# Inputs in 4 KB pieces and transposes of 32-bit token pairs in a recurrent gate kernel

## The chip, the cores and the metric

The kernel runs on one core of one Trainium2 chip. The metric is device time in microseconds, as the median of the executions of one kernel. Each execution carries a state: in these single-core runs, "slow" marks one that is more than 1.5% above the fastest of the same kernel. Ratios below are the mean time of one kernel's fast runs over that of the other kernel's fast runs of the same rounds, on the same chip; so they are not quite the ratio of the medians that stand beside them.

## The reference

Four sequences of 6336 tokens, 256 channels, all in float32. Cut to what matters:

```
a    = exp(8 * sigmoid(r_gate) * log(sigmoid(a_param)))     # decay
norm = sqrt(max(1 - a*a, 1e-6))
xg   = norm * sigmoid(i_gate) * x
h_t  = a_t * h_(t-1) + xg_t                                 # scan over tokens
gate = sigmoid(causal 5-tap convolution of h)
out  = (gate * (h @ w_val)) @ w_out
```

## The kernel before

Tokens come in chunks of 1024 (two tiles of 512). Loads lay tokens on the partitions; the scan needs channels there. So ACT takes tanh of the two gates; DVE or POOL (GpSimd) forms u = (1 + tanh i) * x, called u2 in the text; PE transposes the r half; ACT takes exp of it to give `a`; POOL squares `a` ("e"); ACT takes the root ("sq", several chunks at once); PE transposes the norm back to tokens (nT); DVE multiplies it with u (xg); PE transposes that (xT); and DVE scans it. Loads and stores go on SyncE's queue (called the load queue here), the small weights on GpSimd's software queue.

```
U2 = "PDPDDDDDDPDPDPDPDDPDPPPPPPPPPPPPPPPDPPPPPPPDPPPPPPP"   # who makes u2 of each tile: POOL or DVE
...
def load(c):       # r in pieces of 4 KB (j tokens side by side), i in pieces of 1 KB; x like i
    nc.sync.dma_start(ri[:, 0, 0:nw, 0:nj, :], rf[...].rearrange("(w p j) d -> p w j d", w=nw, j=nj))
    nc.sync.dma_start(ri[:, 1, ...], if_[...].rearrange("(k p) d -> p k d", p=P))
...
nc.vector.tensor_scalar(out=wo[:], in0=wo[:], scalar1=0.5, ...)          # setup, DVE's last instruction there
...
def op_u2(g, eng):
    xt, ti = live["xt", c][:, w * nj:(w + 1) * nj, :], tring[:, NTR + g % NTI, 0:nj, :]
    u = uring[:, g % NU, 0:nj, :]
    if eng == "DVE":
        nc.vector.scalar_tensor_tensor(out=u, in0=ti, scalar=1.0, in1=xt, op0=ALU.add, op1=ALU.mult)
        return
    nc.gpsimd.tensor_scalar(out=t1, in0=ti, ...)                         # t1 = 1 + tanh, f32
    nc.gpsimd.tensor_tensor(out=u, in0=t1, in1=xt, op=ALU.mult)
...
def op_nT(g, eng):                                                       # 8 bf16 transposes a tile
    for h in range(H):
        for j in range(nt // P):
            nc.tensor.transpose(out=nT[:, j, h*P:(h+1)*P], in_=nring[:, h, n0+j*P:n0+(j+1)*P], identity=ident_b[:])
```

The order of the instructions on each engine isn't written down: a small planner in the kernel simulates the engines with a table of costs (`COST`, us per operation) and emits the operations in order of their planned start.

## Time and profile before

| | before |
|---|---|
| median of the 3 runs | 319.87 us (317.4 to 322.94) |
| profiled span, granted clock | 317.1 us, 0.973 |
| ACT busy / idle | 290.1 / 27.0 us |
| POOL busy; in the 120 us from 120 to 240 us | 224.6 us; 114.3 us, 95% |
| share of the load queue (all 16 engines' span) | 91.8% |

The busy table, the stretches, the groups and the windows of the DMA are shown in the prediction. The view of the tile ring that holds u (duration in ns: least/median/most; then first and last start in us):

```profile
L404 DVE TENSOR_TENSOR uring<-bank,uring x51: 398/684/695, 14.6 to 306.2; 128x1024 bf16<-128x1024 bf16 x48, 128x512 bf16<-128x512 bf16 x3
L364 POOL TENSOR_TENSOR uring<-t,xt x36: 1264/2366/3320, 11.3 to 290.2; 128x1024 bf16<-128x1024 f32 x33, 128x512 bf16<-128x512 f32 x3
L360 DVE SCALAR_TENSOR_TENSOR uring<-tring,xt x15: 1198/1381/2480, 24.3 to 265.8; 128x1024 bf16<-128x1024 bf16 x15
```

The first xg starts at 14.6 us: until then DVE has nothing of the main loop to do: it waits for PE's first transposes of the norm, not for `wo`. Then two rows of the waits (engine, line, what it waited for; us in total, times, longest):

```profile
DVE uring L404 <- PE bank L397: 11.6, 15, 4.1
...
DVE wo L313 <- DMA wo<-in_moe_w_out_dram: 7.1, 1, 7.1
```

The second is the setup's scaling of the output weights `wo`. DVE works in order, so everything behind it waits as well.

### The profile page before, as it was taken

The page shows a single profiled execution, that of the slowest core. Times are in us where ns is not written, and L with a number is a line of the kernel's source. Part 1 is how long each engine was busy: PE and PEld are TensorE (multiplying, and loading weights), DVE is VectorE, ACT ScalarE, POOL GpSimd, SP SyncE. Part 2 cuts the span into 40 slices and gives each one's busy share as a digit, 9 for nine tenths or more (in the row PEclk, how much of TensorE's full clock was granted, in tenths as well). Part 3 has the DMA queues.
Part 4 walks back from the last instruction along what each step waited for, and adds up shares of the span by engine and source line. Part 5 has one row for each costly group of instructions (what it writes and reads, how often), then busy time and mean ns, then how long its engine had stood idle before and what let it go on. Part 6 is the DMA issues. An engine that isn't in the chain of part 4 may idle for free.

```text
span 317.1 us, 7227 instructions
## 1 busy us (share of the span) xinstructions
PE 246.2 (78%) x2987; PEld 163.6 (52%) x2987; DVE 270.4 (85%) x269; ACT 290.1 (91%) x231; POOL 224.6 (71%) x140
## 2 busy tenths in 40 slices
PE   1262877687679768897989798959977997999994
PEld 1141745453546446564655375627644665655662
DVE  3125799999597998999999999997998999999892
ACT  6789999899969999999998999899989999998963
POOL 6329551869469536999989999999997289868000
PEclk9999999999759999999999999997999999999997
DMA  8999999999999999999999999996999994853334
GB/s 208 340 365 380 367 368 382 386 345 352 394 322 349 389 356 375 350 391 385 357 382 382 393 369 383 393 389 191 395 385 383 385 379 164 262 189 133 135 154 179
DMA packets 67327, 104.55 MB, mean 330 GB/s; under 512 B 3287, under 2 KB 54238, under 8 KB 67294
## 3 DMA queue, kind: packets, MB, share of 16 engines
q1 hardware_dynamic: 65904, 103.82, 91.8%
q0 software_dynamic: 1376, 0.26, 1.0%
q8 instruction: 23, 0.38, 0.5%
q14 instruction: 10, 0.08, 0.1%
q10 hardware_dynamic: 14, 0.01, 0.0%
HBM read 78.39 MB, written 25.95 MB: 329 GB/s over the span
## 4 chain that ended last, share of the span: by engine, by line
ACT 25%; DMA 23%; DVE 21%; PE 13%; issue 10%; POOL 4%; SPq 1%; DVEq 0%; ACTq 0%; POOLq 0%
DMA ri<-in_i_gate_dram 15%; DVE yring L425 9%; ACT tring L351 8%; DMA xt<-in_x_dram 6%; DVE gv L477 5%; ACT ering L388 5%; PE bank L489 4%; ACT tg L459 4%; ACT aring L376 4%; PE gp L451 3%; DVE osb L500 3%; PE bank L397 3%; POOL uring L364 2%; DMA ri<-in_r_gate_dram 2%; DVE uring L404 2%
## 5 line engine op out<-in xcount | busy, mean ns | idle before, releaser
L384 POOL TENSOR_TENSOR ering<-aring 128x1024 f32<-128x1024 f32 (+2 forms) x56 | 97.1, 1753 | 55.0 <-ACT aring L376 52.8
L425 DVE TENSOR_TENSOR_SCAN yring<-aring,yring,bank 128x1024 bf16<-128x1024 f32 (+5 forms) x54 | 110.1, 2052 | 0.7 <-PE bank L332 0.5
L351 ACT ACTIVATE tring<-ri 128x2048 bf16<-128x2048 f32 (+1 forms) x51 | 93.9, 1868 | 7.8 <-DMA ri<-in_i_gate_dram 7.7
L364 POOL TENSOR_TENSOR uring<-t,xt 128x1024 bf16<-128x1024 f32 (+1 forms) x36 | 83.6, 2323 | 9.9 <-DMA xt<-in_x_dram 7.3
L451 PE MATMUL gp<-yring,diag 64*64 64x512 bf16 (+14 forms) x1196 | 67.9, 350 | 6.7 <-ACT tg L459 4.6
L489 PE MATMUL bank<-wo,gv 128*128 128x256 bf16 x396 | 57.3, 279 | 18.5 <-DVE gv L477 8.2
L477 DVE SCALAR_TENSOR_TENSOR gv<-tg,val 128x1024 bf16<-128x1024 bf16 (+1 forms) x54 | 60.3, 1120 | 6.7 <-ACT tg L459 4.5
L376 ACT ACTIVATE aring<-bank,khf 128x1024 f32<-128x1024 bf16 (+2 forms) x56 | 59.6, 1111 | 3.3 <-PE bank L332 2.5
L459 ACT ACTIVATE tg<-gp 128x1024 bf16<-128x1024 f32 (+1 forms) x51 | 51.1, 1003 | 7.1 <-PE gp L451 6.8
L489 PEld LDWEIGHTS <-gv 128*128 128x128 bf16 x396 | 36.0, 99 | 37.9 <-issue 16.4
L467 PE MATMUL val<-yring,wv 128*128 128x512 bf16 (+1 forms) x204 | 51.5, 376 | 0.8 <-DVE gv L477 0.8
L500 DVE COPY osb<-bank 128x512 f32<-128x512 f32 x69 | 45.6, 679 | 3.8 <-PE bank L489 3.3
L451 PEld LDWEIGHTS <-diag 64*64 64x64 bf16 x1196 | 30.9, 108 | 33.0 <-issue 16.5
L388 ACT ACTIVATE ering<-ering,b 128x2048 bf16<-128x2048 f32 (+4 forms) x15 | 46.7, 3112 | 0.3
L332 PE MATMUL bank<-ident_b,tring 128*128 128x128 bf16 x396 | 31.3, 231 | 18.5 <-ACT tring L351 13.0
L397 PE MATMUL bank<-ident_b,ering 128*128 128x128 bf16 x396 | 32.9, 240 | 15.8 <-ACT ering L388 12.5
L404 DVE TENSOR_TENSOR uring<-bank,uring 128x1024 bf16<-128x1024 bf16 (+1 forms) x51 | 33.4, 669 | 11.8 <-PE bank L397 11.6
L363 POOL TENSOR_SCALAR t<-tring 128x1024 f32<-128x1024 bf16 (+1 forms) x36 | 40.1, 1115 | 2.6 <-ACT tring L351 1.2
L397 PEld LDWEIGHTS <-ering 128*128 128x128 bf16 x396 | 28.1, 108 | 23.3 <-ACT ering L388 15.5
L332 PEld LDWEIGHTS <-tring 128*128 128x128 bf16 x396 | 25.7, 103 | 27.7 <-ACT tring L351 15.1
L332 PE MATMUL bank<-ident_b,uring 128*128 128x128 bf16 x396 | 30.4, 226 | 3.3 <-DVE yring L425 1.8
L360 DVE SCALAR_TENSOR_TENSOR uring<-tring,xt 128x1024 bf16<-128x1024 bf16 x15 | 24.4, 1624 | 8.2 <-DMA xt<-in_x_dram 8.2
(32 smaller groups left out, 112.6 us busy)
## 6 DMA issues: line engine op xcount, KB each, us to landing
out_dram<-osb SPq DMA_DIRECT2D x48, 512.0 KB, 7.1
ri<-in_r_gate_dram SPq DMA_DIRECT2D x23, 1024.0 KB, 8.1
ri<-in_i_gate_dram SPq DMA_DIRECT2D x23, 1024.0 KB, 11.8
xt<-in_x_dram SPq DMA_DIRECT2D x23, 1024.0 KB, 10.7
ri<-in_r_gate_dram SPq DMA_DIRECT2D x2, 512.0 KB, 5.9
ri<-in_i_gate_dram SPq DMA_DIRECT2D x2, 512.0 KB, 8.1
xt<-in_x_dram SPq DMA_DIRECT2D x2, 512.0 KB, 8.1
ri<-in_r_gate_dram SPq DMA_DIRECT2D x3, 256.0 KB, 2.9
```

Source lines behind the costliest of these rows:

```text
L332: nc.tensor.transpose(out=dst[:, col:col + P], in_=src[:, j, h * P:(h + 1) * P], identity=ident_b[:])
L351: nc.scalar.activation(out=tring[:, r:i + 1:i - r, 0:nj, :], in_=ri[:, :, w, 0:nj, :], func=ACT.Tanh, scale=0.5)
L364: nc.gpsimd.tensor_tensor(out=u, in0=t1, in1=xt, op=ALU.mult)
L376: nc.scalar.activation(out=aring[:, h, a0:a0 + nt].rearrange("c (w p j) -> c w p j", p=P, j=nj), in_=live.pop(("srT", k))[:, 0:nt].rearran ...
L384: nc.gpsimd.tensor_tensor(out=ering[:, h, e0:e0 + nt], in0=a, in1=a, op=ALU.mult)
L388: nc.scalar.activation(out=nring[:, :, 2 * e0:2 * e0 + m], in_=ering[:, :, e0:e0 + m], func=ACT.Sqrt, scale=-0.25, bias=b025[:, 0:1])
L397: nc.tensor.transpose(out=nT[:, j, h * P:(h + 1) * P], in_=nring[:, h, n0 + j * P:n0 + (j + 1) * P], identity=ident_b[:])
L425: nc.vector.tensor_tensor_scan(out=yring[:, h, y0 + c0:y0 + c1], data0=aring[:, h, a0 + c0:a0 + c1], data1=xT[:, c0:c1], initial=0.0 if fr ...
L451: nc.tensor.matmul(out=gp[64 * h:64 * h + 64, m, c0:c1], lhsT=diag[rows, h, kk, rows], rhs=yring[rows, h, src:src + c1 - c0], start=(sh == 0),
L459: nc.scalar.activation(out=tg[:, :, 0:nt], in_=live.pop(("gp", g))[:, :, 0:nt], func=ACT.Tanh, scale=0.5)
L477: nc.vector.scalar_tensor_tensor(out=gv[:, 0:nj, hs, :].rearrange("c j h p -> c j (h p)"), in0=tg[:, hs, 0:nt].rearrange("c h (p j) -> c j ...
L489: nc.tensor.matmul(out=ops[:, e * D:(e + 1) * D], lhsT=gv[:, 2 * i + e, hk, :], rhs=wo[:, hk, :], start=(hk == 0), stop=(hk == H - 1))
```

## The change

The intent: i_gate and x, too, come in pieces of 4 KB. Then one partition holds four neighbouring tokens, and a pair of neighbouring bf16 tokens can be taken as one 32-bit word: half as many transposes, in f32, and no copying. For this u must hold the two tokens of a pair side by side, while tanh and x lie token by token. The change lets u2 do the interleaving: it reads both its inputs with hops (512 or 1024 bytes at every element) and writes in a row. The core of the diff:

```diff
-COST = dict(load=(0.05, 2.8), loadx=(0.02, 1.5), ..., u2P=(0.25, 3.15), u2D=(0.2, 1.55), ..., store=(0.05, 1.3))
+COST = dict(load=(0.05, 2.72), loadx=(0.02, 1.37), ..., u2P=(0.25, 3.4), u2D=(0.3, 1.75), ..., store=(0.05, 1.33))
...
-        nc.sync.dma_start(xt[:, 0:nt // P, :], xf[...].rearrange("(k p) d -> p k d", p=P))
+        nc.sync.dma_start(xt[:, 0:nw, 0:nj, :], by_token(xf, c))      # "(w p j) d -> p w j d"; i_gate likewise
...
+            xt = live["xt", c][:, w, 0:nj, :].rearrange("p (w e) d -> p w d e", e=2)
+            u = uring[:, g % NU, 0:nj * D].rearrange("p (w d e) -> p w d e", d=D, e=2)
             if eng == "DVE":
-                nc.vector.scalar_tensor_tensor(out=u, in0=ti, scalar=1.0, in1=xt, ...)
+                tk = ti.rearrange("p (w e) d -> p w d e", e=2)
+                for k in range(nj // 2):
+                    nc.vector.scalar_tensor_tensor(out=u[:, k], in0=tk[:, k], scalar=1.0, in1=xt[:, k], ...)
...
-            nc.gpsimd.tensor_tensor(out=u, in0=t1, in1=xt, op=ALU.mult)
+            nc.gpsimd.tensor_tensor(out=u, in0=t1.rearrange("p (w e) d -> p w d e", e=2), in1=xt, op=ALU.mult)
...
-                for j in range(nt // P):
-                    nc.tensor.transpose(out=nT[:, j, h*P:(h+1)*P], in_=nring[:, h, ...], identity=ident_b[:])
+                for w in range(nw):
+                    nc.tensor.transpose(out=nT[:, w*D + h*P:...], in_=ering[:, h, n0 + w:n0 + nw*P:nw], identity=ident_f[:])
```

The transposes of xg (xT) change in the same way. The table of costs is edited along with it.

More of the change, by code (lines that the diff above doesn't have):

```diff
@@ L36 @@
 U2 = "PDPDDDDDDPDPDPDPDDPDPPPPPPPPPPPPPPPDPPPPPPPDPPPPPPP"
-COST = dict(load=(0.05, 2.8), loadx=(0.02, 1.5), tanh=(0.2, 1.7), u2P=(0.25, 3.15), u2D=(0.2, 1.55), srT=(0.05, 0.45), exp=(0.35, 0.86), e=(0.1, 1.8),
+COST = dict(load=(0.05, 2.72), loadx=(0.02, 1.37), tanh=(0.2, 1.7), u2P=(0.25, 3.4), u2D=(0.3, 1.75), srT=(0.05, 0.45), exp=(0.35, 0.86), e=(0.1, 1.8),
             sq=(0.3, 1.71), nT=(0.05, 0.47), xg=(0.1, 0.58), xT=(0.05, 0.45), scan=(0.21, 2.14), conv=(0.2, 1.1), tg=(0.19, 0.83),
             val=(0.02, 0.93), gv=(0.15, 1.07), out=(0.02, 0.47), osbD=(0.68, 0), osbA=(0.59, 0),
-            store=(0.05, 1.3))
+            store=(0.05, 1.33))
 PRIO = dict(load=5.92, loadx=5.97, store=2.53, tanh=6, exp=2.8, sq=0.42, tg=-0.32, srT=-1.6, nT=0.31, xT=3.79,
@@ L242, with by_token @@
     live = {}
+    def by_token(src, c):
+        t0, nt, g0, g1 = chunks[c]
+        return src[t0:t0 + nt, :].rearrange("(w p j) d -> p w j d", w=g1 - g0, p=P)
     def load(c):
@@ L247, in load @@
         ri = inp.tile([P, 2, 2, SUB, D], FP32, name="ri", tag="ri", bufs=NIN)
-        nc.sync.dma_start(ri[:, 0, 0:nw, 0:nj, :], rf[t0:t0 + nt, :].rearrange("(w p j) d -> p w j d", w=nw, j=nj))
-        nc.sync.dma_start(ri[:, 1, 0:nw, 0:nj, :].rearrange("p w j d -> p (w j) d"),
-                          if_[t0:t0 + nt, :].rearrange("(k p) d -> p k d", p=P))
+        nc.sync.dma_start(ri[:, 0:nw, 0, 0:nj, :], by_token(rf, c))
+        nc.sync.dma_start(ri[:, 0:nw, 1, 0:nj, :], by_token(if_, c))
         live["ri", c] = ri
@@ L255, in loadx @@
         t0, nt, g0, g1 = chunks[c]
-        xt = inp.tile([P, 2 * SUB, D], FP32, name="xt", tag="xt", bufs=NX)
-        nc.sync.dma_start(xt[:, 0:nt // P, :], xf[t0:t0 + nt, :].rearrange("(k p) d -> p k d", p=P))
+        nw, nj = g1 - g0, nt // (g1 - g0) // P
+        xt = inp.tile([P, 2, SUB, D], FP32, name="xt", tag="xt", bufs=NX)
+        nc.sync.dma_start(xt[:, 0:nw, 0:nj, :], by_token(xf, c))
         live["xt", c] = xt
@@ L317, with bank @@
         psum = ctx.enter_context(tc.tile_pool(name="psum", bufs=1, space=bass.MemoryType.PSUM))
-        def bank(b, dtype):
+        def bank(b, dtype=FP32):
             return psum.tile([P, WIN * 4 // mybir.dt.size(dtype)], dtype, name=f"bank{b}", tag=f"bank{b}", bufs=1)
@@ L324 @@
         tring = rings.tile([P, NTR + NTI, SUB, D], BF16, name="tring")
-        uring = rings.tile([P, NU, SUB, D], BF16, name="uring")
+        uring = rings.tile([P, NU, SUB * D], BF16, name="uring")
+        uring_w = uring[:].bitcast(FP32)
         yring = rings.tile([P, H, NY * WIN], BF16, name="yring")
-        def transposes(dst, srcs, h):
-            col = 0
-            for src, nj in srcs:
-                for j in range(nj):
-                    nc.tensor.transpose(out=dst[:, col:col + P], in_=src[:, j, h * P:(h + 1) * P],
-                                        identity=ident_b[:])
-                    col += P
         def op_load(g, eng):
@@ L350, in op_tanh @@
             r, i = g % NTR, NTR + g % NTI
-            nc.scalar.activation(out=tring[:, r:i + 1:i - r, 0:nj, :], in_=ri[:, :, w, 0:nj, :], func=ACT.Tanh, scale=0.5)
+            nc.scalar.activation(out=tring[:, r:i + 1:i - r, 0:nj, :], in_=ri[:, w, :, 0:nj, :], func=ACT.Tanh, scale=0.5)
         def op_u2(g, eng):
@@ L356, in op_u2 @@
             w = g - chunks[c][2]
-            xt, ti = live["xt", c][:, w * nj:(w + 1) * nj, :], tring[:, NTR + g % NTI, 0:nj, :]
-            u = uring[:, g % NU, 0:nj, :]
+            xt = live["xt", c][:, w, 0:nj, :].rearrange("p (w e) d -> p w d e", e=2)
+            ti = tring[:, NTR + g % NTI, 0:nj, :]
+            u = uring[:, g % NU, 0:nj * D].rearrange("p (w d e) -> p w d e", d=D, e=2)
             if eng == "DVE":
-                nc.vector.scalar_tensor_tensor(out=u, in0=ti, scalar=1.0, in1=xt, op0=ALU.add, op1=ALU.mult)
+                tk = ti.rearrange("p (w e) d -> p w d e", e=2)
+                for k in range(nj // 2):
+                    nc.vector.scalar_tensor_tensor(out=u[:, k], in0=tk[:, k], scalar=1.0, in1=xt[:, k], op0=ALU.add,
+                                                   op1=ALU.mult)
                 return
@@ L368, in op_srT @@
             srT = bank(banks["srT", k], BF16)
-            transposes(srT, [(tring[:, g % NTR], tiles[g][1] // P) for g in range(*chunks[c][2:])], h)
+            col = 0
+            for g in range(*chunks[c][2:]):
+                for j in range(tiles[g][1] // P):
+                    nc.tensor.transpose(out=srT[:, col:col + P], in_=tring[:, g % NTR, j, h * P:(h + 1) * P],
+                                        identity=ident_b[:])
+                    col += P
             live["srT", k] = srT
@@ L392, in op_nT @@
             c = chunk_of[g]
-            n0, nt = shape.npos[c] + tiles[g][0] - chunks[c][0], tiles[g][1]
-            nT = bank(banks["nT", g], BF16)[:].rearrange("p (j d) -> p j d", d=D)
+            n0, nw = (shape.npos[c] + tiles[g][0] - chunks[c][0]) // 2, tiles[g][1] // P // 2
+            nT = bank(banks["nT", g])
             for h in range(H):
-                for j in range(nt // P):
-                    nc.tensor.transpose(out=nT[:, j, h * P:(h + 1) * P],
-                                        in_=nring[:, h, n0 + j * P:n0 + (j + 1) * P], identity=ident_b[:])
+                for w in range(nw):
+                    nc.tensor.transpose(out=nT[:, w * D + h * P:w * D + (h + 1) * P],
+                                        in_=ering[:, h, n0 + w:n0 + nw * P:nw], identity=ident_f[:])
             live["nT", g] = nT
         def op_xg(g, eng):
-            nj = tiles[g][1] // P
-            u = uring[:, g % NU, 0:nj, :]
-            nc.vector.tensor_tensor(out=u, in0=live.pop(("nT", g))[:, 0:nj, :], in1=u, op=ALU.mult)
+            n = tiles[g][1] // P * D
+            u = uring[:, g % NU, 0:n]
+            nc.vector.tensor_tensor(out=u, in0=live.pop(("nT", g))[:].bitcast(BF16)[:, 0:n], in1=u, op=ALU.mult)
         def op_xT(k, eng):
             c, h = k // 2, k % 2
-            xT = bank(banks["xT", k], BF16)
-            transposes(xT, [(uring[:, g % NU], tiles[g][1] // P) for g in range(*chunks[c][2:])], h)
+            xT = bank(banks["xT", k])
+            at = 0
+            for g in range(*chunks[c][2:]):
+                nw = tiles[g][1] // P // 2
+                for w in range(nw):
+                    nc.tensor.transpose(out=xT[:, at + w:at + nw * P:nw],
+                                        in_=uring_w[:, g % NU, w * D + h * P:w * D + (h + 1) * P], identity=ident_f[:])
+                at += nw * P
             live["xT", k] = xT
@@ L422, in op_scan @@
             yp = yend(c) - 1
-            xT = live.pop(("xT", k))
+            xT = live.pop(("xT", k))[:].bitcast(BF16)
             for (c0, c1, fresh) in shape.segments(t0, nt):
@@ L485, in op_out @@
             gv = live["gv", g]
-            ops = bank(banks["out", q], FP32)
+            ops = bank(banks["out", q])
             for e in range(2):
```

## The prediction

> **What bounds the kernel now.** I read the page's busy table first, then the busy time of each engine in stretches of 20 us, then the DMA view of two short windows, then the groups, and the chain of waits last.
>
> ```profile
> span 317.1 us, 7227 instructions
> ...
> PE 246.2 (78%) x2987; PEld 163.6 (52%) x2987; DVE 270.4 (85%) x269; ACT 290.1 (91%) x231; POOL 224.6 (71%) x140
> ```
>
> Four engines are near full on average. Only ACT is so full that its own work nearly is the time: 317.1 - 290.1 = 27.0 us idle. The stretches say when (columns: busy us of PE, weight loads, DVE, ACT, POOL; then granted clock, DMA share, GB/s).
>
> ```profile
> core 0: us, PE busy (x) PEld busy (x) DVE busy (x) ACT busy (x) POOL busy (x), PEclk, DMA share, GB/s
> 0.00:20.00 20.00, 6.07 (x47) 3.77 (x47) 5.45 (x23) 14.44 (x16) 10.02 (x18) 1.00 1.02 296
> ...
> 60.00:80.00 20.00, 14.94 (x180) 8.76 (x180) 18.16 (x15) 18.11 (x13) 15.63 (x9) 1.00 1.01 358
> 80.00:100.00 20.00, 15.40 (x164) 11.38 (x164) 15.17 (x14) 16.41 (x13) 13.49 (x6) 0.74 1.00 355
> ...
> 180.00:200.00 20.00, 16.74 (x244) 11.77 (x247) 19.13 (x21) 19.62 (x16) 19.23 (x13) 1.00 1.06 383
> ...
> 280.00:300.00 20.00, 19.58 (x228) 11.90 (x217) 18.97 (x18) 18.57 (x22) 9.85 (x11) 1.00 0.37 146
> ```
>
> There are three stages. Up to about 100 us the DMA share is 1.0 while DVE, ACT and POOL all have holes: the transfers bind. From 120 to 260 us DMA is still full, and ACT, DVE and mostly POOL are at 18 to 20 of 20: everything is balanced, nothing alone binds. After 265 us the loads are over and ACT, DVE and PE drain the queue. ACT's idle time, added up over all the stretches, is 5.6 us before 20 us, 10.1 us after 280, and 11.2 us between; 5.5 of those 11.2 lie between 60 and 100.
>
> Why the transfers bind shows when two windows are put side by side, one moving nearly only i_gate and x (46 to 49 us), one nearly only r_gate and stores (145 to 148 us):
>
> ```profile
> DMA packets 985, 1.06 MB, mean 352 GB/s; under 512 B 16, under 2 KB 964, under 8 KB 985
> ```
>
> ```profile
> DMA packets 401, 1.23 MB, mean 410 GB/s; under 512 B 26, under 2 KB 130, under 8 KB 400
> ```
>
> Both windows are full. The first moves pieces of 1 KB (985 packets for 1.06 MB), the second mostly pieces of 4 KB. The large ones go 16% faster. The chain of waits gives DMA 23%, ACT 25%, DVE 21%, PE 13%; its longest pieces are loads of 7 to 13 us.
>
> The groups that the change touches:
>
> ```profile
> L364 POOL TENSOR_TENSOR uring<-t,xt 128x1024 bf16<-128x1024 f32 (+1 forms) x36 | 83.6, 2323 | 9.9 <-DMA xt<-in_x_dram 7.3
> ...
> L397 PE MATMUL bank<-ident_b,ering 128*128 128x128 bf16 x396 | 32.9, 240 | 15.8 <-ACT ering L388 12.5
> L404 DVE TENSOR_TENSOR uring<-bank,uring 128x1024 bf16<-128x1024 bf16 (+1 forms) x51 | 33.4, 669 | 11.8 <-PE bank L397 11.6
> ...
> L332 PE MATMUL bank<-ident_b,uring 128*128 128x128 bf16 x396 | 30.4, 226 | 3.3 <-DVE yring L425 1.8
> L360 DVE SCALAR_TENSOR_TENSOR uring<-tring,xt 128x1024 bf16<-128x1024 bf16 x15 | 24.4, 1624 | 8.2 <-DMA xt<-in_x_dram 8.2
> ```
>
> **What the Trainium skill says.** (1) "DMA: Bandwidth & Descriptors", section "Why small descriptors are slow (HBM only)", gives each packet a fixed cost of about 3 cycles beside one cycle per 32 bytes. Estimate from it: 4 x (32 + 3) = 140 cycles for four 1 KB pieces, 128 + 3 = 131 for one of 4 KB, 7% apart. The trace agrees in sign and shows more, 352 against 410; I use the trace. (2) "Vector Engine (DVE) Microarchitecture Reference", section "5.2 Measured stream behaviour on trn2 (trn3 not measured)": a two-input stream takes 1.054 ns per column when contiguous and 1.76 when both sources hop at every element. The contiguous half agrees: the fastest call at L360 took 1198 ns for 1024 columns (the row's per-tile view gives 1198/1381/2480 as least, median and most). No run yet shows the hopping half. (3) "SBUF — State Buffer", section "Who interferes with whom": a DVE instruction with two SBUF inputs contends with a POOL instruction that reads SBUF. L360 is such an instruction; its mean of 1624 against its least of 1198 fits. (4) "TensorE: Matmul & The Clock Gate", section "Weight-path perf modes": the fast weight load is not used for FP32. The trace can't show that on 128x128 yet; its only f32 weight loads are three tiny ones of the setup.
>
> **The change, part by part.**
>
> Loads. i_gate and x are 26 MB each, 52 MB together; they go from 1 KB to 4 KB pieces. 52 MB at 352 GB/s is 148 us, at 410 it is 127: at most 21 us of full queue. r_gate and stores already move 4 KB. The kernel's own cost table (its entries agree with the trace's rows to some 2% for scan, gv, tanh and exp) is lowered less: 3.02 to 2.76 us per MB of x and 5.65 to 5.49 for r and i together, about 380 GB/s. Between 12 and 21 us less transfer, then. Per tile of 512 tokens (four pieces of 0.524 MB) DMA falls from 2 x 0.524/0.410 + 2 x 0.524/0.352 = 5.5 us to 5.1 (5.5 by the table's 380). ACT needs 290.1 / 49.5 tiles = 5.9 us per tile. DMA therefore stops binding, but ACT stands right behind it: the gain is limited to ACT's idle time, not to the transfer time saved.
>
> tanh. Same 128x2048 elements, now in one run. Nothing (1919 ns stays).
>
> u2 on DVE, 15 tiles. One instruction of 1024 columns becomes two of 512, both inputs hopping 512 or 1024 bytes at every element. Estimate from page (2): 2 x (512 x 1.76 + about 130) = 2.06 us, where 130 is 1198 - 1024 x 1.054, rounded up for the start. The cost table says 2.05. From 1.62, that is +0.45 us each, 15 x 0.45 = +7 us of DVE. By the order of instructions most of these sit in the first 20 tiles, where DVE idles for transfers; I put 1 us on the path.
>
> u2 on POOL, 36 calls. Same instructions, with hops. No row gives the cost; the table adds 0.25 us per full tile, 36 x 0.25 = +9 us. Most fall between 120 and 240 us, where POOL is 95% busy. A P tile costs POOL 1.16 + 2.42 + 1.96 = 5.5 us (the t, u and e groups), then about 5.8, level with ACT's 5.9. It eats slack; perhaps 1.5 us on the path.
>
> Transposes. The order of instructions shows 396 + 396 bf16 transposes with as many weight loads become 198 + 198 f32 ones, each one instruction in the program; srT stays. In the chain eight bf16 ones take 0.45 to 0.61 us, 56 to 76 ns apart. Without fast load, and with 4-byte words, I expect 110 to 150 ns each: a group of four then costs the same 0.45 to 0.6 us. Total 396 x 130 = 51 us against 792 x 66 = 52. Zero, with the largest uncertainty of the list. The multiplication from PSUM (L404) reads the same bytes through a bf16 view: unchanged at 0.68.
>
> Sum for the path: of the 11.2 us of ACT's holes in the middle I expect about 8.5 back, since loads run ahead; minus 1 for DVE and 1.5 for POOL; start and tail unchanged. Net -6 to -7. The median before is 319.87, so about 313.
>
> **Rivals.** First: transfers are hidden behind the balance anyway. The stretch 180 to 200 speaks for it: ACT at 19.6, DVE at 19.1, POOL at 19.2. Then only the holes up to 100 us come back, and dearer u2 takes most of it: 317 to 320. Second: the f32 transposes are dear. If a 32-bit transpose costs four times a bf16 one (250 ns), PE gains some 50 us of work; it is 17.5 us busy of 20 from 120 us on, and DVE already waits 11.6 us for L397: 325 to 335. Against it: the setup's f32 transposes show one matmul record each, of 233 to 254 ns[...], and the cost table leaves both transposes unchanged. Third: POOL becomes the bound in the middle, if hops cost it 1 us rather than 0.25: 35 us more, 320 to 325. Fourth, on the good side: fewer PE instructions (5972 to 4495 rows) shorten the handovers between PE and DVE, and all 11 us come back: 306 to 308.
>
> **Range and chances.** Centre 313. The good rivals end near 306, the mild bad ones near 321; the repeats before alone span 317.4 to 322.94. 2% faster means below 313.5, almost at my centre, so faster and same share nearly all: 0.5 and 0.43. Slower needs the second or third rival in full: 0.07.
>
> **What would show it.** Full windows at 380 to 410 GB/s, hardly any packets under 2 KB, and the loads ending near 250 instead of 262 us: the loads' step. ACT still near 290 busy with fewer than 7 us of holes between 20 and 280: the main step. DVE u2 near 1.0 us per half, POOL's u near 2.65; f32 transposes in groups of four within 0.6 us. I am wrong if ACT's middle holes stay at 11 us while DMA share falls well below 1 (another engine took over), if PE shows over 90%, or if u2 on POOL exceeds 3 us.

## The result, and the profile after

| | before | after |
|---|---|---|
| median | 320.99 us (317.4 to 322.94, 4 runs) | 375.45 us (373.84 to 376.15, 4 runs) |
| ratio of fast runs | | 1.1733, 95% interval 1.1615 to 1.1852 |
| profiled span, clock | 317.1 us, 0.973 | 374.4 us, 0.922 |
| share of the load queue | 91.8% | 73.0% |

The output is correct, and the time is 17% longer. The busy table of the changed kernel:

```profile
span 374.4 us, 6453 instructions
...
PE 264.4 (71%) x2561; PEld 170.2 (45%) x2591; DVE 291.0 (78%) x284; ACT 292.1 (78%) x231; POOL 272.6 (73%) x140
```

No engine looks full. (PE lacks some records of matmuls here: 2561 beside 2591 weight loads.) ACT does the same work as before (292.1 against 290.1 us) and now idles for 82 us instead of 27. POOL gained 48 us of work, DVE 21. The stretches tell what the averages hide (columns as in the prediction):

```profile
120.00:140.00 20.00, 14.87 (x159) 8.90 (x158) 17.37 (x16) 17.21 (x12) 18.34 (x8) 0.89 0.53 210
140.00:160.00 20.00, 15.39 (x147) 10.13 (x148) 20.00 (x17) 13.82 (x12) 19.66 (x11) 0.91 0.99 360
...
200.00:220.00 20.00, 8.49 (x67) 5.30 (x67) 7.24 (x9) 10.54 (x6) 19.50 (x10) 0.75 0.64 241
...
280.00:300.00 20.00, 12.65 (x119) 7.41 (x120) 15.60 (x13) 17.21 (x13) 19.57 (x9) 0.79 0.78 301
300.00:320.00 20.00, 17.05 (x165) 11.45 (x167) 17.25 (x17) 17.15 (x14) 19.57 (x10) 0.86 0.47 161
```

The last busy column is POOL: from 140 to 320 us it is 18.0 to 19.7 of 20, while PE, DVE and ACT have holes and, outside the stretches from 140 to 200 us, the DMA share is well below 1. From 200 to 220 us POOL is full, PE and DVE stand for more than half of the time and ACT for almost half (9.5 us). The granted clock of TensorE fell too, from 0.973 to 0.922. No run varies it alone; PE is busy for 8.5 to 18.0 of 20 us between 120 and 320 us, so it is not the full engine, but what the lower clock adds is not shown. POOL's work in the ring of u:

```profile
L412 DVE TENSOR_TENSOR uring<-bank,uring x51: 402/682/695, 22.7 to 348.3; 128x1024 bf16<-128x1024 bf16 x48, 128x512 bf16<-128x512 bf16 x3
L367 POOL TENSOR_TENSOR uring<-t,xt x36: 1951/3833/4230, 11.0 to 334.4; 128x1024 bf16<-128x1024 f32 x33, 128x512 bf16<-128x512 f32 x3
L362 DVE SCALAR_TENSOR_TENSOR uring<-tring,xt x30: 678/1384/4252, 21.4 to 295.4; 128x512 bf16<-128x512 bf16 x30
```

POOL's multiplication takes 3833 ns in the median, against 2366 before: in sum 134.1 us against 83.6. DVE's half, 512 columns, takes 678 ns at best and 4252 at most. And the first xg starts at 22.7 us rather than 14.6. How POOL's lateness reaches the other engines is a piece of the timeline (start us, duration us, engine, line; in brackets the idle time before it and what ended it; rows in between are left out):

```profile
201.49 3.74 POOL L367 TENSOR_TENSOR uring<-t,xt 128x1024 bf16<-128x1024 f32 x1
...
205.19 3.74 POOL L392 TENSOR_TENSOR ering<-aring 128x1024 f32<-128x1024 f32 x2
...
208.96 5.42 ACT L396 ACTIVATE ering<-ering,b 128x6144 bf16<-128x6144 f32 x1 [10.37 <-POOL ering L392]
210.02 3.73 POOL L367 TENSOR_TENSOR uring<-t,xt 128x1024 bf16<-128x1024 f32 x1
...
214.43 1.98 PE L405 MATMUL bank<-ident_f,ering 128*128 128x128 f32 x8 [9.47 <-ACT ering L396]
...
215.67 0.69 DVE L412 TENSOR_TENSOR uring<-bank,uring 128x1024 bf16<-128x1024 bf16 x1 [10.84 <-PE bank L405]
```

POOL's squares (L392) stand in order behind its u2. ACT's root of a whole batch (L396) waits 10.37 us for the last square, PE's transposes wait 9.47 us for the root, DVE's xg waits 10.84 us for them. Summed over the run, and with the wait of the start:

```profile
DVE uring L412 <- PE bank L405: 33.6, 14, 11.1
...
PE bank L405 <- ACT ering L396: 19.7, 7, 9.5
...
DVE wo L318 <- DMA wo<-in_moe_w_out_dram: 14.9, 1, 14.9
```

The first was 11.6 us before, the last 7.1. What the change was made for did happen. A full window (110 to 113 us, DMA share 1.03) moves 318 packets, none of the new loads below 4 KB, at 412 GB/s:

```profile
DMA packets 318, 1.24 MB, mean 412 GB/s; under 512 B 16, under 2 KB 16, under 8 KB 318
```

But the transfers then wait for buffers that POOL frees late, and the queue's share falls to 73.0%. The waits of the queue itself show it, for the loads of x before and after:

```profile
SPq L257 <- POOL uring L364: 17.0, 4, 10.4
```

```profile
SPq L262 <- POOL uring L367: 49.0, 12, 9.3
```

### The profile page after: what moved, and what is told of

Read it like the earlier page. It is cut to its first block, busy times and chain, and to the rows that moved or that the text cites. A ratio compares the mean times of both kernels' runs of the same rounds, so it can differ in the third digit from the quotient of the medians.

```text
span 374.4 us, 6453 instructions
## 1 busy us (share of the span) xinstructions
PE 264.4 (71%) x2561; PEld 170.2 (45%) x2591; DVE 291.0 (78%) x284; ACT 292.1 (78%) x231; POOL 272.6 (73%) x140
## 4 chain that ended last, share of the span: by engine, by line
DVE 31%; issue 17%; POOL 17%; PE 16%; DMA 10%; ACT 8%; SPq 0%; DVEq 0%; POOLq 0%; ACTq 0%
DVE yring L439 10%; POOL uring L367 9%; DVE gv L491 7%; DVE uring L362 7%; DMA ri<-in_i_gate_dram 6%; PE gp L465 4%; DMA wo<-in_moe_w_out_dram 4%; PE bank L503 4%; POOL ering L392 4%; DVE osb L514 4%; ACT ering L396 3%; DVE uring L412 3%; PE bank L405 3%; POOL t L366 2%; PE val L481 2%
## 5 line engine op out<-in xcount | busy, mean ns | idle before, releaser
L367 POOL TENSOR_TENSOR uring<-t,xt 128x1024 bf16<-128x1024 f32 (+1 forms) x36 | 134.1, 3725 | 4.6 <-DMA xt<-in_x_dram 1.7
L392 POOL TENSOR_TENSOR ering<-aring 128x1024 f32<-128x1024 f32 (+2 forms) x56 | 95.8, 1736 | 53.6 <-ACT aring L384 52.6
L465 PE MATMUL gp<-yring,diag 64*64 64x512 bf16 (+14 forms) x1196 | 73.9, 374 | 11.7 <-ACT tg L473 9.1
L503 PE MATMUL bank<-wo,gv 128*128 128x256 bf16 x396 | 60.3, 290 | 22.7 <-DVE gv L491 15.8
L503 PEld LDWEIGHTS <-gv 128*128 128x128 bf16 x396 | 38.0, 103 | 44.7 <-DVE gv L491 23.2
L405 PE MATMUL bank<-ident_f,ering 128*128 128x128 f32 x198 | 37.0, 328 | 28.6 <-ACT ering L396 19.7
L396 ACT ACTIVATE ering<-ering,b 128x2048 bf16<-128x2048 f32 (+4 forms) x15 | 46.7, 3112 | 10.9 <-POOL ering L392 10.6
L481 PE MATMUL val<-yring,wv 128*128 128x512 bf16 (+1 forms) x174 | 48.9, 388 | 6.9 <-DVE gv L491 4.8
L465 PEld LDWEIGHTS <-diag 64*64 64x64 bf16 x1196 | 33.2, 115 | 42.4 <-issue 29.1
L375 PE MATMUL bank<-ident_b,tring 128*128 128x128 bf16 x396 | 32.4, 232 | 22.0 <-ACT tring L350 15.8
L362 DVE SCALAR_TENSOR_TENSOR uring<-tring,xt 128x512 bf16<-128x512 bf16 x30 | 46.0, 1573 | 0.6 <-ACT tring L350 0.6
L405 PEld LDWEIGHTS bank<-ident_f,ering 128*128 128x128 f32 x198 | 29.5, 209 | 37.3 <-ACT ering L396 17.9
L421 PE MATMUL bank<-ident_f,uring 128*128 128x128 f32 x198 | 33.6, 303 | 10.8 <-DVE uring L412 8.6
```

Of the source, the lines that this page charges most:

```text
L362: nc.vector.scalar_tensor_tensor(out=u[:, k], in0=tk[:, k], scalar=1.0, in1=xt[:, k], op0=ALU.add, op1=ALU.mult)
L367: nc.gpsimd.tensor_tensor(out=u, in0=t1.rearrange("p (w e) d -> p w d e", e=2), in1=xt, op=ALU.mult)
L375: nc.tensor.transpose(out=srT[:, col:col + P], in_=tring[:, g % NTR, j, h * P:(h + 1) * P], identity=ident_b[:])
L392: nc.gpsimd.tensor_tensor(out=ering[:, h, e0:e0 + nt], in0=a, in1=a, op=ALU.mult)
L405: nc.tensor.transpose(out=nT[:, w * D + h * P:w * D + (h + 1) * P], in_=ering[:, h, n0 + w:n0 + nw * P:nw], identity=ident_f[:])
L465: nc.tensor.matmul(out=gp[64 * h:64 * h + 64, m, c0:c1], lhsT=diag[rows, h, kk, rows], rhs=yring[rows, h, src:src + c1 - c0], start=(sh == 0),
```

## The experiments

Two theories stood at first. H: POOL's hopping reads are the loss. D: DVE's hopping reads, in two halves, are. Later came W (the 32-bit transposes), S (4 KB loads delay `wo`), P (DVE's split), R (only the read side of the hop costs) and O (the order that the edited table plans). Of the 18 kernels, nine give wrong results (u in another order than the transposes expect, or the like; the same amount of work). The profiles of three (e6, e20, e23) are of slow runs; from these only durations of single instructions, counts, sums of busy time and shares are taken, no time of the whole. "The old order" is that of before.

### Hops taken out, on both engines or on one

e1: u2 in natural order on both engines (wrong result). e2: on POOL alone. e3: on DVE alone (both wrong).

```diff
-nc.gpsimd.tensor_tensor(out=u, in0=t1.rearrange("p (w e) d -> p w d e", e=2), in1=xt, op=ALU.mult)
+nc.gpsimd.tensor_tensor(out=un, in0=t1, in1=xn, op=ALU.mult)        # e1, e2: rows as they lie
-    nc.vector.scalar_tensor_tensor(out=u[:, k], in0=tk[:, k], scalar=1.0, in1=xt[:, k], ...)
+    nc.vector.scalar_tensor_tensor(out=un[:, 2*k:2*k+2], in0=ti[:, 2*k:2*k+2], ..., in1=xn[:, 2*k:2*k+2], ...)   # e1, e3
```

> The changed kernel, but DVE and POOL multiply the gated input in its natural order (no hops); the words transposed then hold the wrong pairs, so the values are wrong on purpose. Theory H (the hopping reads of u2 on POOL are the cause, DVE's extra time is mostly waiting for POOL): POOL u back to 2.4 us, a DVE half at 0.7 to 0.8 us, time 315 to 328 us. Rival W (32-bit transposes, their waits, the new order): the time stays above 350 us with u back at 2.4 us.

> Only POOL in natural order, DVE still hops (wrong values on purpose). Theory H: POOL u 2.4 us, and the DVE half falls from 1.57 to about 1.0 us though its own code is as it was, since POOL holds shared reads for less time; time 320 to 335 us. Rival D (DVE's own hops are what costs): the DVE half stays near 1.5 us and the time above 350 us.

> Only DVE in natural order, POOL still hops (wrong values on purpose). Theory H: POOL u stays 3.7 to 3.9 us, DVE half still above 1.2 us on average, time 360 to 374 us. Rival D: time below 345 us.

Measured (views of the ring as above, first two rows e2, then e3):

```profile
L369 POOL TENSOR_TENSOR uring<-t,xt x36: 1268/2362/2904, 10.4 to 307.8; 128x1024 bf16<-128x1024 f32 x33, 128x512 bf16<-128x512 f32 x3
L362 DVE SCALAR_TENSOR_TENSOR uring<-tring,xt x30: 674/702/2867, 20.5 to 271.9; 128x512 bf16<-128x512 bf16 x30
...
L370 POOL TENSOR_TENSOR uring<-t,xt x36: 1952/3832/4193, 10.1 to 333.7; 128x1024 bf16<-128x1024 f32 x33, 128x512 bf16<-128x512 f32 x3
L365 DVE SCALAR_TENSOR_TENSOR uring<-tring,xt x30: 664/1342/4244, 21.1 to 294.5; 128x512 bf16<-128x512 bf16 x30
```

Times: e1 345.17 us (a fast run of 339.44 and a slow one of 350.90), e2 351.52 (ratio 1.0917), e3 375.34 (1.1657), beside 322.31 for before. POOL's u2 falls to 2.33 us a call in e1 and e2 and stays at 3.72 in e3. So taking DVE's hops away alone gives nothing clear of the noise; taking POOL's away alone gives 24 us. D falls. In e3 DVE's halves lie in rows and still take 1549 ns in the mean, up to 4244; in e2 they hop and take 1280, with a median of 702. A half takes as long as it must stand beside POOL, not as long as it hops: its longest is 4.2 us when POOL's calls last 3.9 and 2.8 to 2.9 when they last 2.4. But H missed as well: it had expected e1 at 315 to 328. Fast run against fast runs, some 17 us are lost elsewhere.

### Hops put in, alone

e4: the kernel before with nothing changed but u2's reads and, with them, DVE's two halves (wrong result).

```diff
-u = uring[:, g % NU, 0:nj, :]
+u = uring[...].rearrange("p (w d e) -> p w d e", ...)   # both inputs "p (w e) d -> p w d e"; DVE in two halves
```

> The kernel before with nothing of the change but the hopping order of u2 on both engines (wrong values on purpose): 1 KB loads and bf16 transposes stay. Theory H: POOL u 3.7 to 3.9 us, time 355 to 370 us, most of the loss without any other part of the change. Rival W: below 335 us.

Measured: 360.0 us, ratio 1.118. POOL's calls of a full tile take 3841 ns. Two stretches of it, columns as before:

```profile
180.00:200.00 20.00, 13.99 (x144) 7.77 (x144) 14.82 (x14) 11.88 (x9) 19.66 (x11) 0.91 0.93 326
...
260.00:280.00 20.00, 12.83 (x118) 7.42 (x119) 14.77 (x13) 12.87 (x10) 19.75 (x10) 0.91 1.06 382
```

The picture of the changed kernel, POOL full and the others with holes, comes from the hops alone (with DVE's split): +38 us, with the old loads, the old transposes and the old order.

### The other two parts, alone

e6: before with 4 KB loads only (wrong result: tokens permuted). e13: before with 32-bit transposes only (wrong result).

```diff
-... .rearrange("(k p) d -> p k d", p=P)            # i_gate and x
+... .rearrange("(w p j) d -> p w j d", ...)        # e6
-nT, xT: 8 bf16 transposes a tile, ident_b
+nT, xT: 4 f32 transposes a tile, ident_f           # e13
```

> The kernel before with i_gate and x loaded as 4 KB pieces and nothing else changed (tokens land elsewhere, wrong values on purpose). If the loads were worth what the prediction said: 308 to 316 us. Theory S (4 KB pieces in front of the small weight transfers delay the landing of wo, for which DVE waits in order): the first wait of DVE on wo grows from 7 to about 14 us, and the time is 320 to 328 us, or splits in two groups some 8 to 11 us apart.

> The kernel before with only the transposes of norm and u replaced by half as many 32-bit ones, u left in its natural order (wrong values on purpose), 1 KB loads. Theory H: the 32-bit groups of four take about what eight bf16 ones took, time 316 to 326 us. Rival W: their longer weight loads and matmuls (209 and 328 ns on average in the changed kernel against 108 and 240) delay DVE, time 330 to 345 us.

Measured: e6 with fast runs of 314.72 and 317.01 (and slow ones of 319.8 and 322.63), ratio 0.9865, interval 0.978 to 0.9951. The load queue's share falls from 91.8% to 85.6%. e13 322.25, ratio 1.0065. So the loads give back about 4 us by the fast runs (over all runs the medians are 318.4 and 320.04: unclear), the words cost 2: W falls. And `wo` landed 5.8 us after issue in e6's one profile, against 7.7 before: 4 KB pieces as such need not delay it, S falls in that form.

### The same interleaving done by the write

e5 (correct result): the reads go along the rows, the write goes to every second bf16.

```diff
+un = uring[...].rearrange("p (w d e) -> p w e d", d=D, e=2)      # inputs "p (w e) d -> p w e d", in rows
-nc.gpsimd.tensor_tensor(out=u, in0=t1.rearrange("p (w e) d -> p w d e", e=2), in1=xt, op=ALU.mult)
+nc.gpsimd.tensor_tensor(out=un, in0=t1.rearrange("p (w e) d -> p w e d", e=2), in1=xn, op=ALU.mult)
```

> The changed kernel, with the two tokens of a word interleaved when u is written instead of when its inputs are read: both engines read 256 elements in a row and write every second bf16. Right values. Theory R (only a hop on the reads costs POOL): POOL u near 2.4 us, time 335 to 350 us like the run with natural order. Rival T (any hop costs POOL, written ones too): POOL u above 3 us, time above 355 us.

Measured: 352.2 us, ratio 1.0997, and POOL's rows (view of the groups: count, busy us, mean ns, idle before):

```profile
L372 POOL TENSOR_TENSOR uring<-t,xt 128x1024 bf16<-128x1024 f32 x33 | 79.5, 2408 | 2.8
L365 DVE SCALAR_TENSOR_TENSOR uring<-tring,xt 128x512 bf16<-128x512 bf16 x30 | 37.0, 1284 | 0.6 <-ACT tring L350 0.6
```

A full tile takes 2408 ns, the 2419 of before: on POOL a write that steps over every second bf16 is free and only the hopping read costs (R stands). The time still lies 32 us above before: the missing part is not in POOL's u2.

### What kind of hop

e23: the changed kernel in the old order, with POOL's u2 of three kinds, by tile number (wrong result).

```diff
+if g % 3 == 0:   # x hops, t1 is read in a row                                (line 372)
+elif g % 3 == 1: # t1 hops, x is read in a row                                (line 375)
+else:            # both hop, but in runs of two neighbouring 4-byte words      (line 378)
```

> Wrong output on purpose, same work: the changed kernel in the old order, with GpSimd's u2 of three kinds by tile number: only x read with hops, only the tanh term read with hops, both read with hops but two neighbouring words at a time. Natural takes 2.3 to 2.4 us a full tile, both hopping 3.7 to 3.9. If each hopping source costs the same, the first two kinds take 3.0 to 3.2; if one source of either kind is enough for the whole cost, 3.7 to 3.9; if only distance at every single word costs, the third is 2.4 to 3.1, if any hop costs in full 3.7 to 3.9.

Measured: 330.33 us (fast runs 325.99 and 328.56, ratio 1.0187). The tile view of the three lines, from a slow run:

```profile
L372 POOL TENSOR_TENSOR uring<-t,xt x14: 1409/2648/2997, 11.3 to 298.6; 128x1024 bf16<-128x1024 f32 x13, 128x512 bf16<-128x512 f32 x1
L378 POOL TENSOR_TENSOR uring<-t,xt x12: 1509/2830/3144, 35.2 to 309.9; 128x1024 bf16<-128x1024 f32 x11, 128x512 bf16<-128x512 f32 x1
L375 POOL TENSOR_TENSOR uring<-t,xt x10: 1399/2648/2989, 90.9 to 306.5; 128x1024 bf16<-128x1024 f32 x9, 128x512 bf16<-128x512 f32 x1
```

All the expectations for one source missed: one hopping source, whichever, costs 0.3 us a tile (2.65 us in the median against the 2.37 of before), not 0.7 and not 1.4. Two sources that hop by pairs of words cost 0.5. Only two sources that hop at every single word cost 1.5 (3.83). The least values, all of the tiles half as large, say the same: 1.40, 1.51 and 1.95, against 1.27 in rows.

### The order

e12: natural order on both engines, DVE in one instruction, order of after (wrong result). e14: e1 in the order of before, that is with before's table of costs (wrong). e15: the changed kernel whole in the order of before (correct).

```diff
-nc.vector.scalar_tensor_tensor(...)   # twice, half a tile each
+nc.vector.scalar_tensor_tensor(...)   # e12: once
-COST = ...   # table of after
+COST = ...   # e14, e15: table of before; nothing else
```

> As the run with natural order on both engines (order of instructions of the changed kernel, wrong values on purpose), but DVE multiplies a tile in one instruction of 1024 columns instead of two of 512. Theory P (what is left over 322 us comes from DVE waiting twice for POOL per tile): u2 of DVE falls from 2 x 1.25 to about 1.6 us and the time to 322 to 332 us. Theory O (it comes from the new order of instructions, which the altered cost table gives, and from wo's late landing): 337 to 351 us as before.

> Natural order of u2 on both engines in two DVE halves (wrong values on purpose), with the cost table of the kernel before, so that the instructions stand in the order of before. Theory O: wo lands after 6 to 8 us and the time is 318 to 328 us. Theory P: 335 us or more.

> The changed kernel whole, with hops, right values; only its cost table is that of before, so that the order of instructions is that of before. Hops alone in the kernel before gave 360 us, loads alone -4, words alone +2: if these add and the rest was order, 355 to 362 us. If the order counts for nothing: 366 to 376 us.

Measured: e12 347.3, e14 327.35 (fast runs only: mean 326.81, ratio 1.0233), e15 360.93 (1.1277, interval 1.114 to 1.1415, wholly below the 1.1615 to 1.1852 of after). Joining DVE's halves gives nothing in the new order (e1's one fast run 339.44, e12 344.79 to 347.79): P falls there. Fast runs against fast, the old order gives 12.6 us (from e1) to 20 (from e12) to the natural kernel and 14.5 to the changed one (375.45 to 360.93). The new order is a loss of its own; it is not the hops in another guise, since it is about as large where no read hops. e14 and e15, of the same rounds, differ in the hops alone: 34 us.

### What the order does at the start

In the new order x of the second chunk is loaded ahead of r and i of the third; the load queue's share between 5 and 10 us is then 82.9% rather than 75.9%, and the small pieces of the weights on the software queue come through later. Between 5 and 10 us the software queue (q0: packets, MB, share) moved, before and after:

```profile
q0 software_dynamic: 1205, 0.22, 52.2%
```

```profile
q0 software_dynamic: 768, 0.10, 29.8%
```

In the changed kernel `wo` landed 15.4 us after issue, against 7.7. Over all profiles: in the order of before (with either half of e24 and e25 counted by its start) 5.8 to 8.6 us in nine, and 11.6 and 15.8 in two, both slow runs; in the order of after 11.8 to 15.9 us in eight and 7.0 in one, e1's run of 339 us, whose second run, not profiled, took 351. So the order makes a late landing likely, not certain. (No kernel has the new order without 4 KB loads; of the eight profiles with 4 KB loads in the old order six landed early, so the order counts beyond the loads.) e8: `wo` scaled just before its first use instead of in the setup (correct). e22: that, and u2 of the second tile, which e8 had left waiting for x ahead of the first xg, moved behind the first tile's gated value (correct).

```diff
-nc.vector.tensor_scalar(out=wo[:], in0=wo[:], scalar1=0.5, ...)         # setup
 def op_out(q, eng):
+    if q == 0:
+        nc.vector.tensor_scalar(out=wo[:], in0=wo[:], scalar1=0.5, ...)  # e8, e22
+order: u2 of tile 1 behind gv of tile 0                                  # e22
```

> The changed kernel with DVE's scaling of wo moved from the setup to just before the first product that needs it, so that DVE doesn't wait for wo's landing ahead of its first tiles. Right values. Theory S: 364 to 369 us, 7 to 11 us less than 375.5. Rival (POOL alone sets the time, a late start is made up for): 373 to 376 us.

> Correct output: the changed kernel with its hops and its new order, but DVE's scaling of the output weights just before their first use and the second tile's u2 placed behind the first tile's gated value. If the new order costs only by its start, 359 to 363 (as the changed kernel in the old order, 360.9). If only the 7 us of the start come off and the rest of the order costs the other half, 366 to 370. First scan at 15 us rather than 23.

Measured: e8 368.24 (ratio 1.1502), e22 370.42 (1.1554), both below the 375.45 of after, though by 7 and 5 us only (the better of the two is the one with the late u2; the difference of 2 us isn't explained). e22 starts its first xg at 14.6 us, as before does, although `wo` lands 15.3 us after issue: the start is repaired, and half of the 14.5 us at most came off.

### Where else the order costs

e24: planned with the old table up to the planned 60 us, with the new one after. e25: the other way round (both correct).

```diff
+if t >= 60.0:
+    dur = later[op][i][1]        # duration from the other table
```

> Correct output: the changed kernel, its order of instructions planned with the cost table of before up to the planned 60 us and with the changed table after that. If the new order costs only by its first 60 us, 359 to 363, as the changed kernel in the old order; if the rest of the order costs as much as the start, 366 to 369; if the start is nothing, 374 to 377. The output weights land by 9 us.

> Correct output: the same the other way round, the changed table up to the planned 60 us and the table of before after that. If the first 60 us are the cost, 373 to 377; if both halves cost, 366 to 369; if only the rest costs, 359 to 363. Output weights at 15 us. If both this run and its counterpart lie near 361 or both near 375, the order's cost is no sum of stretches and stays open.

Measured: e24 367.22 (1.1434), e25 368.67 (1.1484). Between old/old 360.93 and new/new 375.45, then, the later part costs 6.3 us alone and the first part 7.7 (5.0 and 6.6 by the ratios); within the noise they add up to the 14.5. Which displacement after 60 us does it, no run tells.

### Versions that might have won

e16 (correct): u with tokens innermost, one DVE instruction, old order. e20 (correct): e5 in the old order. e21 (correct): e20 with seven of DVE's fifteen tiles given to POOL.

```diff
+u = uring[...].rearrange("p (d j) -> p j d", j=nj)           # e16
-U2 = "PDPDDDDDDPDPDPDPDDPDPPPPPPPPPPPPPPPDPPPPPPPDPPPPPPP"
+U2 = "PDPDPDPDPPDPPPDPPDPDPPPPPPPPPPPPPPPPPPPPPPPPPPPPPPP"   # e21
```

> Right values: 4 KB loads and 32-bit transposes kept; u lies with its tokens innermost (column by column), so that both engines read whole rows and write with a step, DVE in one instruction per tile; order of instructions as before. POOL u near 2.4 us, DVE u2 near 1.6 us. If hops, split and order were all that was wrong: 312 to 320 us, a little under the kernel before. If the stepped writes of the transposes to PSUM or of u cost: 325 us or more.

> Correct output: the changed kernel with rows read as they lie and the pairs interleaved by the write, in the order of instructions of the kernel before. If the hopping reads and the order are the whole cost, it is the natural-order kernel of this order (327.35 us) within 2%: 321 to 333. If the write with steps costs something in this order, or the order's 14 us do not come off here, 340 to 352. GpSimd's u2 2.3 us a call, DVE's halves 1.3 to 1.5 us.

> Correct output: the same with seven of the fifteen DVE tiles of u2 moved to GpSimd (DVE about -19 us of work, GpSimd about +24). If DVE is what limits once the hops are gone, 313 to 322; if GpSimd is still the limit in the middle, 330 to 345, with GpSimd over 19 of 20 us busy from 120 us on.

Measured: e16 330.06 (1.0344), e20 327.9 (fast runs 322.79 and 327.45, ratio 1.0119, interval 0.9989 to 1.025), e21 339.32 (1.0575). e20 is the changed kernel without both of its losses, and it comes out level with before or a little above (verdict unclear). It isn't shown to win. DVE's u2 costs more there, 37.6 us against 24.4, as its halves stand beside POOL one by one; giving seven tiles to POOL takes 15 us off DVE and puts 22 on POOL, which is 19.0 to 19.6 of 20 us busy from 140 to 220 us: 14.5 us worse, fast runs against fast. In e16 the write of u goes to every fourth bf16. That costs DVE 2884 ns a tile in the mean and 2429 at least (1624 and 1198 before), POOL 2597 in the mean (2419 before).

## Why the prediction was wrong

The predicted time was 313 us, between about 306 and 321, with 0.07 for slower. It took 375.45. By its steps:

**u2 on POOL: the step that failed.** It read: "No row gives the cost; the table adds 0.25 us per full tile, 36 x 0.25 = +9 us." and "It eats slack; perhaps 1.5 us on the path." Measured is +1.46 us per full tile (2419 to 3884), +50 us in all. A hypothesis of whoever edited the cost table was taken for a measurement. And the page that states the cost was missed: "GPSIMD Engine Reference", section "7. Performance pitfalls for Q7 kernels", says that reads with a step over 8 bytes take about 2.9 rather than 1.9 cycles per element, half as much again. The page says it of kernels written for GpSimd's own cores; that a built-in instruction pays as well is what the trace shows. An estimate from the page is 2.42 x 0.5 = 1.2 us a tile, 43 us in all. The trace shows 60% more per full tile, so the page is near.

The second half of the step failed too, on what was in sight. The prediction itself said that most of these calls lie where POOL is 95% busy. Its own sum for a P tile, with 3.88 for 2.42, gives 1.16 + 3.88 + 1.96 = 7.0 us, against ACT's 5.9: POOL becomes the bound. On a full engine an addition isn't slack eaten: 29 of the 36 calls of before start after 120 us, at 2320 ns in the mean (the groups of that stretch alone); the changed kernel's calls there take 3733 ns, and 29 x 1.41 us are 41 us. Measured on the time are 38 us for the hops of both engines (e4, with DVE's split), 34 (e15 against e14), and 24 for POOL's alone in the new order (e2): about half to three quarters of the 50 us added to POOL, not all of it. The third rival had this mechanism right, with 1 us a call for its size. But it put the result at only 320 to 325, though its own 35 us of work would have met the same full engine.

**"Start and tail unchanged".** Wrong at the start. The order costs 14.5 us, of which 5 to 7 come off when DVE is kept from waiting for `wo` (e8, e22); the rest of the order costs some 6 us after the planned 60 us (e24). The prediction had looked at the order of instructions for the place of DVE's u2, but not at the order of the transfers against the small weights. No rival contained it.

**Loads.** The mechanism was right: full windows run at 412 GB/s (380 to 410 were predicted). The size was off by half: about 4 us on the path (e6's fast runs) instead of 8.5. Its reading of the stages was also too broad: from 20 to 60 us ACT was busy for 19.7 and 19.9 of 20, so the transfers did not hold it up there, and from 200 to 220 us the DMA share was 0.90, from 240 to 260 us POOL was busy for 11.1.

**u2 on DVE.** +7 us of work was predicted; it is +21.6 (24.4 to 46.0). But hops are not the reason: the best half takes 678 ns hopping and 664 in rows (e3), so the 1.76 ns per column taken from (2) did not show. It's the time beside POOL's longer calls, and it shrinks with them.

**Transposes.** Zero was predicted, 2 us measured (e13). Right: a group of four takes 0.60 to 0.75 us in most places of the timeline, little more than expected, and the weight loads of xT 141 ns in the median against 98 in bf16, which fits (4). The count in the fourth rival was not: the profiles have 5974 PE records before and 5152 after (some 30 more with the missing ones), not 5972 and 4495.

**Its own tests.** It would be wrong "if ACT's middle holes stay at 11 us while DMA share falls well below 1 (another engine took over)" or "if u2 on POOL exceeds 3 us". Both came true, the first beyond its wording: ACT's holes between 20 and 280 us, added up over the stretches as in the prediction, are 50 us.

**The sum.** Loads -1.35%, words +0.65%, hops with DVE's split +11.8% make 11.1%; the changed kernel in the old order is at +12.8%, and the natural kernel in that order at +2.3%, where loads and words alone would make -0.7%. That remainder, 5 to 10 us, stays open. DVE's halves are the suspect, as they take 41.4 us in e14 against 24.4; but one instruction in natural order was run only with the new order, so it isn't shown. A correct kernel with 4 KB loads and bf16 transposes would be the natural successor of e6; no run here is one.

## What to carry to other kernels

Before an interleaving is put into an instruction, ask which engine executes it and where that engine is full: the cost belongs on the side, read or write, source by source, where that engine takes it for free, and on a full engine much of what is added reaches the time (24 to 38 of 50 us here). An average of 71% hid a stretch at 95%. And when a planner derives the order from a table of costs, an edit of that table is a change of its own, to be run alone.

## What the Trainium skill lacked or had wrong

- "GPSIMD Engine Reference", "7. Performance pitfalls for Q7 kernels": the surcharge of about 50% for reads with steps over 8 bytes is near what two hopping sources cost (60%: 2.42 to 3.88 us per tile of 1024 columns). The page does not say that it depends on the number of sources: with one hopping source of two it was 2.65 us in the median (2.37 before), about 12%, and with both hopping by pairs of words 2.83. Nor does it say that a write to every second bf16 is free (2.41 in the mean, against 2.42).
- "Vector Engine (DVE) Microarchitecture Reference", section "5.2 Measured stream behaviour on trn2 (trn3 not measured)": its 1.76 ns per column for two hopping sources, measured on 32-bit data that hop over regions of 4 KB, did not show for a bf16 source with an f32 one that each alternate between two rows: 678 ns for 512 columns hopping, 664 in rows. The page itself notes that a one-source stream alternating between two regions ran at the full rate; whether the types or the two rows make the difference, no run tells.
- "SBUF — State Buffer", section "Who interferes with whom", agrees and could give a size: a DVE instruction with two SBUF inputs and 0.68 us of work took up to 4.25 us beside POOL calls of 3.9 us, and up to 2.9 us beside calls of 2.4.
- "TensorE: Matmul & The Clock Gate" gives no duration for a 32-bit transpose of 128x128. Here the weight load of xT took 137 to 141 ns (least and median) and its matmul record 272 to 273, against 95 to 98 and 216 to 219 in bf16. Where the weights are every second word instead of neighbours (nT; xT too in e16) the load's median was 209; half as many transposes cost the kernel 0.65% (e13).
- "DMA: Bandwidth & Descriptors", section "Queues, rings and completion order", says that an engine takes turns between its queues packet by packet, but gives no delay for small transfers beside a full load queue: 128 KB of weights in two transfers landed 5.8 to 8.6 us after issue in most profiles of one order of loads, and 11.8 to 15.9 us in most of another.
